# A gated linear attention and a bilinear feed-forward on one core: zero matmuls at the start, half products at the head of two chunks, and a query load behind a gate

## The chip, the cores and the metric

The kernel runs on one core of a Trainium2 chip. The metric is the device time of one launch in microseconds. The kernel of before has a median of 196.31 us over three runs (195.17, 196.31 and 201.79).

The engines are named as the profile names them: PE is TensorE (matmuls) and PEld its weight loads, DVE is VectorE, ACT is ScalarE, POOL is GpSimd, SP is SyncE. POOL, SP and ACT also issue DMA transfers. Each engine runs its own queue of instructions in order and waits at an instruction until what that needs is there.

## The reference

Two stages follow each other. The first is a recurrence over 768 steps for each of 4 batch rows and 8 heads, with a state of 48 x 48:

```python
for t in range(S):
    state = alpha[:, :, t, :, None] * state + np.einsum('bhd,bhe->bhde', k[:, :, t], v[:, :, t])
    y[:, :, t] = np.einsum('bhd,bhde->bhe', q[:, :, t], state)
```

The second takes the 3072 tokens of 384 features and computes `((x @ w_a) * (x @ w_b)) @ w_out`, with an inner width of 1536.

## The kernel before

**Chunks.** The recurrence is cut along time. A chunk is 256 steps of two batch rows: chunk c covers the steps of c // 2 and the batch rows c % 2 * 2 and the next one, so there are six chunks, 0 to 5. Inside a chunk the two batch rows are u = 0 and u = 1, and steps are held in even and odd pairs on 128 partitions.

**Stages of a chunk.** The gates' logarithms (`ln`, L411) are summed over time on TensorE with a triangular matrix: chunk 0 with `B` (L453), chunk 1 with `A2` (L503), the later ones with `AQ` (L498), which takes the sums in three bf16 parts; the parts come from `lx` (L424, L427) and the subtractions `R 0` and `R 1` (L488) on VectorE. ScalarE turns the sums into the decays beta and 1/beta (`E`, L532). `lv` (L517) and `mk`, `mq` (L543) multiply keys and queries by them. The result is turned so that the features lie on partitions: on TensorE for the first chunks (`C`, `Ce`), by a DMA transpose that SP issues for the later ones (`T`, L595, into the tile kqT). Then come the states (`K`, `KA`, L618; `k`, L650 to L654), the scores (`D`, L665) with their masks (`Mc` copies on ScalarE, L674, and `Mm` masks in place on VectorE, L678), and the outputs (`SB`, `SA`, `Y`). For chunks 2 to 5 the output leaves PSUM into ys (`X`, L755 or L757) and is turned by a DMA transpose into xT (`XT`, L762), one for each u.

**Feed-forward.** For a chunk's 512 tokens there are 12 slices f of the inner width. `a f` and `b f` (L777) are three matmuls each into one PSUM bank, `as f` (L783) copies the first out on ScalarE, `pr f` (L791) multiplies both on VectorE. Their second argument says which tokens: `*` both batch rows (512 columns), `0` or `1` one of them (256 columns, which read only that u of xT). The last argument of `a` and `b` is the PSUM bank. `o m h` (L799) are the output matmuls of 128 tokens in two halves of the inner width, `ot` copies them out, `st` stores them.

**Order.** No scheduler runs. The string PROGRAM is a hand written list of such operations, each with its chunk ahead of the colon; the kernel issues them in that order, each to its engine, so that the string fixes the order on every queue. In it the feed-forward of one chunk is interleaved with the attention stages of the next one or two. An instruction that writes a PSUM bank waits until the bank's last reader is done. The copies of `as` rotate through three buffers. All eight banks are addressed by number.

**Loads.** GpSimd issues most loads (`ld ... P`, L404) and the weights (`W`, L384; `Wo`, L387) in the order of the string, with its own small multiplications `lv ... P` between them. SP issues the first loads, the transposes, the stores, and small transfers of decays (`dr`, `dl`, L549, L554).

The operations `fill n i` (n matmuls of 128 x 128 by 512 zero columns into bank i, L437), `c1` (memsets of the zero tile wz and of og, L328 to L331), and `gatet u` (a GpSimd copy of one element of kqT of row u, L851) already exist in the table of operations. Before, `fill` is used twice, with five matmuls behind chunk 0's second sums and with one later, and `gatet` is not used.

Of the kernel before, what the change touches and what calls it, by code (L numbers as in the profile page):

```python
# [14 lines left out]


PROGRAM = """
0: c1a; cz 0 q V; cz 0 b P; cs 0 m P; ci; cz 1 q V; cz 0 v V; ld a 0b Y; ln 0b; cs 0 0 P; cm 0; cu; cu2 P; B 0b 3; Bs 0b; c1; cs 1 m P; ld v 0 P; ld a 1 P
0: cz 1 b P; ld a 0a Y; ln 0a; B 0a 1; Bs 0a; E 0a b; fill 5 2; cus; ld q 0a Y; mq 0a V; E 0b i; ld q 0b Y; ld k 0a Y; ld k 0b Y; mk 0b V; E 0b b; mq 0b V
0: C 0 1 5; E 0a i; mk 0a V; Ce 0 1 V; C 0 0 3; Ce 0 0 V; dk 0 6; fill 1 1; v 0 S; de 0; K 0 0 7; k 0 0 V; ln 1; cs 1 0 P; ld q 1 P; ld k 1 P; W b 0 256  # L20
0: cm 1; ld v 1 P; c2 P; c3 P; D 0 1 5; M 0 1; D 0 0 0; SB 0 6; B 1a 4; Bs 1a; Mc 0 0; Mm 0 0 V; B 1b 5; Bs 1b; E 1a i; E 1a b; mq 1a V; mk 1a V; K 0 1 4; E 1b i
# [117 lines left out]
1: o 0 1 -; ot 0 V; a 1 1 6; a 10 1 1; as 1 1; as 10 1  # L139
3: E 0 b; E 0 i  # L140
1: b 4 1 2; pr 4 1; b 8 1 5; b 1 1 1; a 8 1 6; b 10 1 0; pr 1 1; o 3 0 2; pr 10 1; as 8 1; pr 8 1; o 3 1 -; ot 3 S; st 3 Y
2: a 4 * 7; as 4 *
3: E 1 b
2: a 5 * 6; b 4 * 3
3: E 1 i
1: st 0 Y
3: dr; ld k * P; lv 0 k P; lv 1 k P
4: lx V; R 0
3: mk 0 V; mq 0 V; T 0
4: ld q * Y  # L150
2: a 1 * 2; b 5 * 0; as 5 *; pr 5 *
4: ra 1
2: b 7 * 4; b 10 * 1; pr 4 *; a 10 * 6; as 10 *; pr 10 *
3: mk 1 V
2: a 7 * 0; b 1 * 5; a 0 * 6; b 0 * 7; as 1 *; as 7 *; pr 1 *; pr 7 *; as 0 *; a 3 * 0; b 9 * 1; pr 0 *
3: mq 1 V; ld v * P
5: ld a * P
2: as 3 *; b 3 * 2; a 9 * 6
4: ra 0
2: pr 3 *; as 9 *; pr 9 *; a 2 * 5  # L160
4: lv 0 q P
2: as 2 *; b 2 * 7; pr 2 *
3: KA * 06; D 0 0 4; M 0 0; dl; k * 0 V; k * 1 V
# [21 lines left out]
2: o 2 0 1; o 2 1 -; o 3 0 6; o 1 0 0; o 3 1 -; o 1 1 -  # L185
4: dr
1: st 1 Y
3: a 11 * 5
2: ot 2 V; ot 3 V
4: mq 0 V; mk 0 V  # L190
5: lx V
3: a 9 * 3; a 0 * 2; a 8 * 6; b 11 * 7; as 9 *; as 11 *; as 0 *; pr 11 *; b 9 * 2; b 0 * 1; pr 9 *
5: lv 0 k V
3: as 8 *
2: ot 1 S
3: b 8 * 3; a 5 * 4; as 5 *; a 6 * 6; a 4 * 7; pr 0 *; pr 8 *
5: R 0
4: mq 1 V
3: b 5 * 3; a 1 * 1; pr 5 *; as 4 *; b 6 * 7; as 6 *; pr 6 *
4: ld v * P; K * 0 2; T 0; D 0 1 5  # L200
3: as 1 *
4: D 0 0 3; Mc 0 0; dl; k * 0 V
# [9 lines left out]
4: SB 0 3; SB 1 5; D 1 1 0; Mc 1 1  # L212
3: b 3 * 7; pr 3 *; b 10 * 2
4: D 1 0 0; Mc 1 0; Mm 1 1 V
5: ld q * P; lv 1 q P
3: pr 10 *
4: SA 1; SA 0; Y 0; X 0 S; XT 0
# [738 lines left out]
```

## Time and profile before

| | |
|---|---|
| median of three runs | 196.31 us |
| the profiled execution, its own time | 196.55 us |
| its span | 194.8 us, so 1.75 us lie around it |
| PE busy | 183.4 us, 94% |
| DVE busy | 137.2 us, 70% |
| ACT busy | 103.0 us, 53% |
| POOL busy | 55.8 us, 29% |
| DMA | 30.96 MB, 159 GB/s on average |
| granted TensorE clock | 1.0 |

A row of the timeline gives start, duration, engine, line, operation, what it writes and reads, and in brackets how long the engine had been idle ahead of it and what ended that. A row of the chain that ended last gives start, duration and what held the end at that time. Busy time of PE is modelled, since matmuls are pipelined: the pace is better taken from the start of one group to the start of the next.

### The profile page before, as it was taken

How to read it: one execution, taken by the hardware profiler on the slowest of the kernel's cores; microseconds unless marked ns; L12 is line 12 of the kernel's file. 1: busy time of each engine (PE TensorE's matmuls, PEld its weight loads, DVE VectorE, ACT ScalarE, POOL GpSimd, SP SyncE). 2: the span in 40 equal slices, each digit the busy share in tenths (PEclk: the TensorE clock that was granted, in tenths of full speed). 3: DMA queues.
4: the chain of work that ended last, by engine and by line, in shares of the span. 5: the costliest groups of instructions: out<-in, count | busy, mean ns of one | idle time of the engine just before them, and what ended most of it. 6: DMA issues, size and time to landing. Idle time of an engine off the chain costs nothing.

```text
span 194.8 us, 5851 instructions
## 1 busy us (share of the span) xinstructions
PE 183.4 (94%) x2498; PEld 111.5 (57%) x2498; DVE 137.2 (70%) x230; ACT 103.0 (53%) x189; POOL 55.8 (29%) x75
## 2 busy tenths in 40 slices
PE   1998899899999999999998989999999999999993
PEld 1577675566687877644555534555544556544463
DVE  3588966999899796779979379786755871147520
ACT  4465766686765668555566035766245712154401
POOL 8999734860640424400512400040000000000000
PEclk9999999999999999999999999999999999999999
DMA  5999999999999997999996996566388005013013
GB/s 127 263 214 188 237 231 257 245 247 258 255 228 232 189 252 142 127 267 226 131 237 131 131 277 150 111 51 78 82 156 183 3 3 112 9 43 121 2 40 122
DMA packets 57882, 30.96 MB, mean 159 GB/s; under 512 B 47824, under 2 KB 54880, under 8 KB 57856
## 3 DMA queue, kind: packets, MB, share of 16 engines
q0 software_dynamic: 19680, 18.09, 49.0%
q1 hardware_dynamic: 38032, 12.41, 31.5%
q8 instruction: 19, 0.31, 0.6%
q10 hardware_dynamic: 144, 0.10, 0.2%
q14 instruction: 7, 0.06, 0.1%
HBM read 25.98 MB, written 4.74 MB: 158 GB/s over the span
## 4 chain that ended last, share of the span: by engine, by line
PE 75%; DMA 10%; POOL 8%; issue 2%; DVE 2%; ACT 2%; POOLq 0%; ACTq 0%; DVEq 0%
PE psum L777 43%; PE psum L799 20%; DMA wb_t<-in_moe_w_b_dram 7%; DMA xT<-ys 3%; PE psum L665 3%; PE psum L715 2%; PE psum L618 2%; DVE prod L791 1%; POOL a_t L404 1%; PE psum L498 1%; PE psum L689 1%; PE psum L694 1%; POOL wa_t L384 1%; PE psum L810 1%; POOL v_t L404 1%
## 5 line engine op out<-in xcount | busy, mean ns | idle before, releaser
L777 PE MATMUL psum<-xT,wb_t 128*128 128x512 bf16 (+1 forms) x270 | 57.1, 337 | 0.8 <-DVE prod L791 0.3
L777 PE MATMUL psum<-xT,wa_t 128*128 128x512 bf16 (+1 forms) x270 | 56.1, 337 | 0.7 <-DMA xT<-ys 0.7
L799 PE MATMUL psum<-wo_t,prod 128*128 128x384 bf16 x276 | 48.5, 326 | 0.7 <-issue 0.7
L777 PEld LDWEIGHTS <-wb_t 128*128 128x128 bf16 x270 | 25.6, 98 | 21.6 <-issue 1.1
L777 PEld LDWEIGHTS <-wa_t 128*128 128x128 bf16 x270 | 25.4, 98 | 20.5 <-issue 1.2
L799 PEld LDWEIGHTS <-prod 128*128 128x128 bf16 x276 | 26.2, 98 | 17.6 <-issue 0.7
L517 POOL TENSOR_TENSOR q_t<-q_t,ra 128x384 f32<-128x384 f32 x8 | 9.1, 1135 | 46.8 <-ACT ra L510 32.0
L674 ACT ACTIVATE m<-psum 128x1024 bf16<-128x1024 f32 x16 | 16.2, 1022 | 6.3 <-PE psum L665 6.3
L816 DVE COPY ot<-psum 128x384 f32<-128x384 f32 (+1 forms) x13 | 6.9, 538 | 16.5 <-PE psum L799 14.1
L814 ACT ACTIVATE ot<-psum 128x384 f32<-128x384 f32 (+1 forms) x12 | 5.7, 477 | 12.9 <-PE psum L799 11.9
L678 DVE TENSOR_TENSOR m<-m,mask 128x1024 bf16<-128x1024 bf16 x16 | 11.6, 732 | 0.4 <-ACT m L674 0.4
L543 DVE TENSOR_TENSOR QKp<-k_t,invb 128x768 bf16<-128x768 f32 x10 | 11.1, 1114 | 0.2
L411 ACT ACTIVATE la<-a_t 128x1536 f32<-128x1536 f32 (+2 forms) x9 | 9.5, 1057 | 3.2 <-DMA a_t<-in_alpha_dram 3.1
L670 DVE TENSOR_TENSOR m<-psum,mask 128x1024 bf16<-128x1024 f32 x8 | 9.7, 1218 | 1.6 <-PE psum L665 1.5
L543 DVE TENSOR_TENSOR QKp<-q_t,beta 128x768 bf16<-128x768 f32 x10 | 9.3, 946 | 0.0
L517 POOL TENSOR_TENSOR k_t<-k_t,a_t 128x384 f32<-128x384 f32 x5 | 4.9, 992 | 14.8 <-DMA k_t<-in_k_dram 14.8
L404 POOL DMA_DIRECT2D a_t<-in_alpha_dram x7 | 7.4, 1059 | 5.5 <-DVE prod L791 2.9
L665 PE MATMUL psum<-kqT 64*64 64x128 bf16 x384 | 8.6, 218 | 0.5 <-DVE prod L791 0.2
L453 PE MATMUL psum<-la,ut 128*128 128x192 f32 x16 | 4.7, 448 | 4.2 <-ACT la L411 4.2
L404 POOL DMA_DIRECT2D v_t<-in_v_dram x8 | 8.5, 1066 | 0.1
L665 PEld LDWEIGHTS <-kqT 64*64 64x64 bf16 x384 | 6.4, 107 | 2.9 <-issue 2.5
L755 ACT ACTIVATE ys<-psum 128x768 bf16<-128x768 f32 x7 | 5.6, 809 | 4.3 <-PE psum L694 2.3
(271 smaller groups left out, 274.6 us busy)
## 6 DMA issues: line engine op xcount, KB each, us to landing
out_dram<-ot SPq DMA_DIRECT2D x23, 192.0 KB, 2.6
a_t<-in_alpha_dram POOLq DMA_DIRECT2D x4, 768.0 KB, 11.4
k_t<-in_k_dram POOLq DMA_DIRECT2D x4, 768.0 KB, 8.2
q_t<-in_q_dram POOLq DMA_DIRECT2D x3, 768.0 KB, 10.3
v_t<-in_v_dram POOLq DMA_DIRECT2D x4, 384.0 KB, 6.2
a_t<-in_alpha_dram POOLq DMA_DIRECT2D x3, 384.0 KB, 5.6
q_t<-in_q_dram POOLq DMA_DIRECT2D x3, 384.0 KB, 14.1
k_t<-in_k_dram POOLq DMA_DIRECT2D x3, 384.0 KB, 14.0
```

Of the source, the lines that this page charges most:

```text
L404: eng.dma_start(out=t[:, us, hs].rearrange("p b h r d -> p (b h) (r d)"), in_=src[ch.b0 + us.start:ch.b0 + us.stop, hs, ch.s * 2 * C:(ch.s ...
L411: nc.scalar.activation(out=ch.la[:, us, hs].rearrange("p b h r d -> p (b h r d)"), in_=ch.a[:, us, hs].rearrange("p b h r d -> p (b h r d) ...
L517: eng.tensor_mul(x, x, by)
L543: eng.tensor_mul(QKp[ch.c % 2][:, u, j, :, hs, :D], src[:, u, hs].rearrange("p h r d -> p r h d"), f)
L665: nc.tensor.matmul(s2[g * HC:(g + 1) * HC, r, p, rk, :], lhsT=ch.kqT[u][rs, 1, rk, 2 * h + p, g * HC:(g + 1) * HC], rhs=queriesT(ch, u, 2 ...
L670: nc.vector.tensor_mul(m.rearrange("p r a k s -> p (r a) (k s)"), ch.s2[u, h].rearrange("p r a k s -> p (r a) (k s)"), maskn(4))
L674: nc.scalar.activation(out=m.rearrange("p r a k s -> p (r a) (k s)"), in_=ch.s2[u, h].rearrange("p r a k s -> p (r a) (k s)"), func=AF.Copy)
L678: eng.tensor_mul(x, x, maskn(4))
L777: nc.tensor.matmul(p, lhsT=(wa_t, wb_t)[w][:, kk, f * 128:(f + 1) * 128], rhs=ch.xT[:, us.start // 2:us.stop // 2, kk].rearrange("p u g s ...
L799: nc.tensor.matmul(op, lhsT=ch.prod[:, f, at:at + C], rhs=wo_t[:, f, :], start=(f == 0), stop=(f == NFF - 1))
L814: nc.scalar.activation(out=o_, in_=i_, func=AF.Copy)
L816: eng.tensor_copy(o_, i_)
```

## The change

Three edits, all of them in the string.

1. `c1` moves from behind chunk 0's first sums to the second place of the string, and `fill 7 2` follows it: seven zero matmuls into bank 2 ahead of anything else on TensorE.
2. At the head of chunk 2's feed-forward the products of f = 4, 5 and 1 are made for u = 0 and u = 1 apart, and at the head of chunk 3's those of f = 11, 9 and 0. The bank numbers around them change, and some operations on VectorE change places: `R 0` of chunk 4 goes behind `mq 1` of chunk 3, `lx` of chunk 5 goes behind the first three half products of chunk 3.
3. `gatet 1` of chunk 4 is put on GpSimd's queue ahead of `ld q` of chunk 5.

```diff
-0: c1a; cz 0 q V; cz 0 b P; ... Bs 0b; c1; cs 1 m P; ld v 0 P; ld a 1 P
+0: c1a; c1; fill 7 2; cz 0 q V; cz 0 b P; ... Bs 0b; cs 1 m P; ld v 0 P; ld a 1 P
...
-2: a 4 * 7; as 4 *
+2: a 4 0 7; as 4 0; b 4 0 3
 3: E 1 b
-2: a 5 * 6; b 4 * 3
+2: a 5 0 6; as 5 0; b 5 0 0
 3: E 1 i
 1: st 0 Y
 3: dr; ld k * P; lv 0 k P; lv 1 k P
-4: lx V; R 0
+4: lx V
+2: pr 4 0
 3: mk 0 V; mq 0 V; T 0
 4: ld q * Y
-2: a 1 * 2; b 5 * 0; as 5 *; pr 5 *
+2: a 1 0 5; as 1 0; b 1 0 1; a 4 1 2; b 4 1 3; a 5 1 7; a 1 1 4; pr 5 0; as 4 1; pr 1 0; b 5 1 6; b 1 1 5
 4: ra 1
-2: b 7 * 4; b 10 * 1; pr 4 *; a 10 * 6; as 10 *; pr 10 *
+2: a 10 * 2; as 5 1; b 10 * 1; pr 4 1; pr 5 1; a 7 * 7; as 1 1; as 10 *; pr 1 1; pr 10 *; b 7 * 0; as 7 *
 3: mk 1 V
-2: a 7 * 0; b 1 * 5; a 0 * 6; b 0 * 7; as 1 *; as 7 *; pr 1 *; pr 7 *; as 0 *; a 3 * 0; b 9 * 1; pr 0 *
+2: a 0 * 6; pr 7 *; b 0 * 4; as 0 *; a 3 * 3; b 9 * 5; pr 0 *
 3: mq 1 V; ld v * P
+4: R 0
...
-3: a 11 * 5
+3: a 11 0 5; as 11 0
 2: ot 2 V; ot 3 V
 4: mq 0 V; mk 0 V
+3: b 11 0 7; a 9 0 3; as 9 0; b 9 0 2; a 0 0 4; as 0 0; b 0 0 1; pr 11 0; pr 9 0; pr 0 0
 5: lx V
-3: a 9 * 3; a 0 * 2; a 8 * 6; b 11 * 7; as 9 *; as 11 *; as 0 *; pr 11 *; b 9 * 2; b 0 * 1; pr 9 *
+3: a 11 1 6; as 11 1; b 11 1 7; a 9 1 5; as 9 1; b 9 1 2; a 0 1 3; as 0 1; b 0 1 4; pr 11 1; pr 9 1; pr 0 1
 5: lv 0 k V
-3: as 8 *
+3: a 8 * 6; as 8 *; b 8 * 1; a 5 * 2; as 5 *; a 6 * 3; a 4 * 5; pr 8 *
 2: ot 1 S
-3: b 8 * 3; a 5 * 4; as 5 *; a 6 * 6; a 4 * 7; pr 0 *; pr 8 *
 5: R 0
 4: mq 1 V
-3: b 5 * 3; a 1 * 1; pr 5 *; ...
+3: b 5 * 4; a 1 * 1; pr 5 *; ...
...
 4: D 1 0 0; Mc 1 0; Mm 1 1 V
+4: gatet 1
 5: ld q * P; lv 1 q P
```

More of the change, by code (lines that the diff above doesn't have):

```diff
@@ L17 @@
 PROGRAM = """
-0: c1a; cz 0 q V; cz 0 b P; cs 0 m P; ci; cz 1 q V; cz 0 v V; ld a 0b Y; ln 0b; cs 0 0 P; cm 0; cu; cu2 P; B 0b 3; Bs 0b; c1; cs 1 m P; ld v 0 P; ld a 1 P
+0: c1a; c1; fill 7 2; cz 0 q V; cz 0 b P; cs 0 m P; ci; cz 1 q V; cz 0 v V; ld a 0b Y; ln 0b; cs 0 0 P; cm 0; cu; cu2 P; B 0b 3; Bs 0b; cs 1 m P; ld v 0 P; ld a 1 P
 0: cz 1 b P; ld a 0a Y; ln 0a; B 0a 1; Bs 0a; E 0a b; fill 5 2; cus; ld q 0a Y; mq 0a V; E 0b i; ld q 0b Y; ld k 0a Y; ld k 0b Y; mk 0b V; E 0b b; mq 0b V
@@ L147 @@
 3: dr; ld k * P; lv 0 k P; lv 1 k P
-4: lx V; R 0
+4: lx V
+2: pr 4 0
 3: mk 0 V; mq 0 V; T 0
 4: ld q * Y
-2: a 1 * 2; b 5 * 0; as 5 *; pr 5 *
+2: a 1 0 5; as 1 0; b 1 0 1; a 4 1 2; b 4 1 3; a 5 1 7; a 1 1 4; pr 5 0; as 4 1; pr 1 0; b 5 1 6; b 1 1 5
 4: ra 1
-2: b 7 * 4; b 10 * 1; pr 4 *; a 10 * 6; as 10 *; pr 10 *
+2: a 10 * 2; as 5 1; b 10 * 1; pr 4 1; pr 5 1; a 7 * 7; as 1 1; as 10 *; pr 1 1; pr 10 *; b 7 * 0; as 7 *
 3: mk 1 V
-2: a 7 * 0; b 1 * 5; a 0 * 6; b 0 * 7; as 1 *; as 7 *; pr 1 *; pr 7 *; as 0 *; a 3 * 0; b 9 * 1; pr 0 *
+2: a 0 * 6; pr 7 *; b 0 * 4; as 0 *; a 3 * 3; b 9 * 5; pr 0 *
 3: mq 1 V; ld v * P
+4: R 0
 5: ld a * P
-2: as 3 *; b 3 * 2; a 9 * 6
+2: as 3 *; b 3 * 2; a 9 * 0
 4: ra 0
-2: pr 3 *; as 9 *; pr 9 *; a 2 * 5
+2: pr 3 *; as 9 *; pr 9 *; a 2 * 1
 4: lv 0 q P
@@ L187 @@
 1: st 1 Y
-3: a 11 * 5
+3: a 11 0 5; as 11 0
 2: ot 2 V; ot 3 V
 4: mq 0 V; mk 0 V
+3: b 11 0 7; a 9 0 3; as 9 0; b 9 0 2; a 0 0 4; as 0 0; b 0 0 1; pr 11 0; pr 9 0; pr 0 0
 5: lx V
-3: a 9 * 3; a 0 * 2; a 8 * 6; b 11 * 7; as 9 *; as 11 *; as 0 *; pr 11 *; b 9 * 2; b 0 * 1; pr 9 *
+3: a 11 1 6; as 11 1; b 11 1 7; a 9 1 5; as 9 1; b 9 1 2; a 0 1 3; as 0 1; b 0 1 4; pr 11 1; pr 9 1; pr 0 1
 5: lv 0 k V
-3: as 8 *
+3: a 8 * 6; as 8 *; b 8 * 1; a 5 * 2; as 5 *; a 6 * 3; a 4 * 5; pr 8 *
 2: ot 1 S
-3: b 8 * 3; a 5 * 4; as 5 *; a 6 * 6; a 4 * 7; pr 0 *; pr 8 *
 5: R 0
 4: mq 1 V
-3: b 5 * 3; a 1 * 1; pr 5 *; as 4 *; b 6 * 7; as 6 *; pr 6 *
+3: b 5 * 4; a 1 * 1; pr 5 *; as 4 *; b 6 * 7; as 6 *; pr 6 *
 4: ld v * P; K * 0 2; T 0; D 0 1 5
```

## The prediction

> **What bounds the kernel now.** I read the page's engine shares and clock row first, then the chain of work that ended last in order of time, then the timeline around the three places that are edited, and last the DMA view for the loads that move.
>
> ```profile
> PEclk9999999999999999999999999999999999999999
> PE 75%; DMA 10%; POOL 8%; issue 2%; DVE 2%; ACT 2%; POOLq 0%; ACTq 0%; DVEq 0%
> ```
>
> TensorE carries three quarters of the chain, and the granted clock is full in every slice. The chain in order of time shows where TensorE itself is made to wait:
>
> ```profile
> 17.14 13.55 DMA wb_t<-in_moe_w_b_dram
> 30.69 0.05 issue
> 30.74 1.47 PE psum L777 x6
> ...
> 62.45 5.28 PE psum L777 x48
> ...
> 81.90 11.65 PE psum L777 x54
> ...
> 106.61 6.22 DMA xT<-ys
> 112.83 0.14 issue
> 112.96 9.22 PE psum L777 x42
> ...
> 129.46 0.92 ACT m L674
> 130.38 0.04 issue
> 130.43 0.40 PE psum L665 x14
> ```
>
> Columns are start, duration, what. Up to 30.69 us the chain is loads: the third piece of wb_t, issued at 17.14, sets it. From there on it is matmuls, dense but for a few holes. Two of the holes lie where the change works: the wait for chunk 3's second turned row (to 112.83), and a stretch at 126 to 130.4 where VectorE and ScalarE hold TensorE up. The two L777 rows give the pace: 5.28/48 = 110 ns for a matmul of 256 columns (chunk 1's half products) and 11.65/54 = 216 ns for one of 512.
>
> **Zero matmuls ahead of the first sums.** The memsets of wz and og go to the head of VectorE's queue, and seven 512-column matmuls to the head of TensorE's. The rows of before:
>
> ```profile
> 4.19 2.90 PE L453 MATMUL psum<-la,ut 128*128 128x192 f32 x8 [4.19 <-ACT la L411]
> 6.88 2.15 PE L437 MATMUL psum<-wz 128*128 128x512 bf16 x5
> ```
> ```profile
> 33.87 0.56 DVE L517 TENSOR_TENSOR k_t<-k_t,a_t 128x384 f32<-128x384 f32 x1 [0.85 <-DMA k_t<-in_k_dram]
> ```
>
> TensorE idles until 4.19, and its first matmuls go at half pace although the granted clock reads full: five zero matmuls in 2.15 us are 430 ns each, twice the 216 above, and the first eight sums take 2.90 us. Seven at 430 ns are 3.0 us of the 4.19 idle ones, so they end about when the sums may begin; ahead by a memset, at worst 0.3 us late. If they bring the full pace forward the first sums, and what follows, come half of 2.90, some 1.4 us, sooner (an estimate). I price it at nothing either way. The cover is the 13.55 us row: TensorE still meets wb_t at 30.69, and behind it VectorE meets chunk 1's keys at 33.87, both of them loads that GpSimd issues and that this edit does not touch. The bounds are 0.3 us lost and 1.4 us gained, the latter only if loads do not hold the stage.
>
> [...]
>
> **Row by row products, chunk 2.** Products 4, 5 and 1 of both kinds become halves: six groups of three 512-column matmuls turn into twelve groups of three 256-column ones. Per group split: 6 x 110 - 3 x 216 = +12 ns, so six cost 0.07 us of TensorE. Three evictions on ScalarE and three products on VectorE become six each:
>
> ```profile
> 80.40 0.43 DVE L791 TENSOR_TENSOR prod<-as__1745,psum 128x256 bf16<-128x256 bf16 x1
> ...
> 116.47 0.73 DVE L791 TENSOR_TENSOR prod<-as__2307,psum 128x512 bf16<-128x512 bf16 x1 [1.23 <-PE psum L777]
> ```
>
> That is 2 x 0.43 - 0.73 = 0.13 us on VectorE for each split, some 0.4 in all; ScalarE, with fewer instructions in this stage, pays about the same. It lies beside 11.65 us of dense matmuls. There is no wait of TensorE in front of chunk 2's first product for the split to remove (the dense row starts straight behind the output matmuls), and the row taken first, row 0, is the one whose turn is issued last. Walking the new bank numbers with these durations I find each bank read out before it is written again, the tightest at the scores of chunk 3, whose banks VectorE has free some 0.5 us ahead. R 0 of chunk 4 (one VectorE subtraction) moves behind chunk 3's queries; its reader, chunk 4's quad sums, comes behind all of chunk 2's products. Price 0.07 us; if the cover went, 0.4 us.
>
> **Row by row products, chunk 3.** Here row 0 is turned first.
>
> ```profile
> 103.44 1.99 SPq L762 DMA_TRANSPOSE xT<-ys  x1
> ```
> ```profile
> 112.96 2.75 PE L777 MATMUL psum<-xT,wa_t 128*128 128x512 bf16 x12 [0.68 <-DMA xT<-ys]
> ...
> 128.82 1.50 PE L777 MATMUL psum<-xT,wb_t 128*128 128x512 bf16 x6 [0.33 <-DVE prod L791]
> ...
> 135.38 4.06 PE L799 MATMUL psum<-wo_t,prod 128*128 128x384 bf16 x24
> 139.28 0.81 PE L777 MATMUL psum<-xT,wa_t 128*128 128x512 bf16 x3
> ```
>
> Row 0 is turned from 103.44, row 1 lands at 112.83. The first product reads both and idles 0.68 us; a half product of row 0 does not. TensorE then has six groups (6 x 3 x 110 = 2.0 us) before it needs row 1, which covers it. **Gain 0.68, cost 0.07.** VectorE gains too: it idled 1.23 us until 116.47 because the first second factor came after four first ones; now halves are multiplied at once, its three extra halves (0.4 us) fit into that idle time, and chunk 4's last queries end some 0.8 us sooner. So VectorE keeps step with the earlier TensorE, and I carry the 0.61 through to 126 us.
>
> **Chunk 5's queries behind chunk 4's turned keys.** GpSimd gets a tiny copy that reads chunk 4's second turned tile, and behind it on its queue wait the query load, lv 1 q and the value load of chunk 5, nothing else. Who waits for those: VectorE's lv 0 q and, behind it in order, product 7; later the queries' multiply and the state sums of chunk 5.
>
> ```profile
> 126.05 2.09 DVE L678 TENSOR_TENSOR m<-m,mask 128x1024 bf16<-128x1024 bf16 x2
> ```
> ```profile
> L678 DVE TENSOR_TENSOR m<-m,mask x16: 671/681/1497, 14.0 to 156.6; 128x1024 bf16<-128x1024 bf16 x16
> ```
> ```profile
> 126.16 1.42 POOL L517 TENSOR_TENSOR q_t<-q_t,ra 128x384 f32<-128x384 f32 x1 [16.96 <-ACT ra L510]
> ```
> ```profile
> 121.22 1.94 SPq L595 DMA_TRANSPOSE kqT<-QKp  x1
> 132.64 3.61 SPq L762 DMA_TRANSPOSE xT<-ys  x2
> ```
> ```profile
> kqT<-QKp SPq DMA_TRANSPOSE x2, 4.4
> ```
> ```profile
> q_t<-in_q_dram POOLq DMA_DIRECT2D x1, 768.0 KB, 7.7
> ```
> ```profile
> DMA to landing us min/median/max: 4.3/9.0/15.8
> ```
> ```profile
> 133.42 0.55 DVE L517 TENSOR_TENSOR q_t<-q_t,ra 128x384 f32<-128x384 f32 x1
> 135.65 0.73 DVE L791 TENSOR_TENSOR prod<-as__2470,psum 128x512 bf16<-128x512 bf16 x1 [1.68 <-PE psum L777]
> ```
>
> In times of before: the turn issued at 121.22 lands 4.4 later, at 125.6, and the gate opens; the same load took 7.7 us from issue (the median of query loads is 9.0, the least 4.3, the most 15.8), so the queries land at 133.3. VectorE comes to lv 0 q at 133.42. Product 7 waits for TensorE until 135.65, so lv 0 q may start as late as 135.1: 1.8 us of slack, and no cost.
>
> What it moves is lv 1 q. In before it starts on GpSimd at 126.16, 0.1 us behind two masks on VectorE: the longer took 1497 ns where the median is 681, 0.8 us lost, and product 2 behind them is what TensorE waits for at 128.82 (0.33) and through ScalarE at 130.43. That second wait: six matmuls from 128.82 at 216 ns end at 130.12, the scores start at 130.43, 0.31. With lv 1 q gone to about 133.5 both waits, 0.64 in sum, should go. What is late next is a mask or R 1 near 131 to 134, where its last reader has about 1 us to spare. **Gain between 0 and 0.64; I take 0.5**, as the masks are named by the chain.
>
> [...]
>
> **Sum.** 0.68 - 0.07 - 0.07 + 0.5 = 1.04 us. The profiled execution took 196.55 us, a span of 194.8 and 1.75 around it; the median of the runs is 196.31, 0.24 below it, and its lowest 195.17. 196.55 - 1.04 = 195.5, rounded.
>
> **The rivals.** [...] *The gated load comes late*, the slower side: the point is 135.1 - 125.6 = 9.5 us from issue to landing. Beyond it each microsecond delays lv 0 q, product 7 and TensorE's 24 output matmuls at 135.38, whose eighth (135.38 + 7 x 0.169 = 136.6) reads product 7 (ready 136.4): no slack, one for one. At the median 9.0 nothing happens; at the longest, 15.8, it costs 6.3: 201.8; halfway (12.7) 3.2: 198.7. Against: the queues are quiet then, for it: the median lies only 0.5 below the point. *The value load hits the turns of chunk 4*: behind lv 1 q it is issued at about 134.5, while row 1 is turned from about 135.0. In chunk 3 such a turn beside a value load took 6.22 (106.61 to 112.83) and here it would land at 141.2, 1.9 after 139.28 where TensorE wants it: 197.4. Against: a load's data move some time after its issue, and the turn may be through. *The head pays after all*: the 1.4 us pass 30.7: 194.1. Against: the two loads.
>
> **How the numbers follow.** Forecast 0.42 (own range 194.8 to 196.0), the block moves 0.15, the value load 0.15, the late load 0.17 (0.12 of it beyond +2%, 200.2), the head 0.07, and 0.04 for a gain that no row shows. The range, 193.9 to 198.4, takes in all but most of the late load and the last. Two per cent, 3.9 us, is about what a measurement of this kernel can tell from no change; TensorE's holes after 30.7 us come to less, so faster by over 2% gets 0.04, slower 0.12, within 0.84.
>
> **What would show it.** Right: no wait for xT ahead of chunk 3's first product and VectorE's 1.23 us of idle before its first product there gone; zero matmuls at 1 to 4 us, wb_t still ending at about 30.7; lv 1 q of chunk 5 after 130 us, all masks near 0.68 us at 126, and no wait at the scores of 130.4. Wrong: VectorE waiting for q_t ahead of lv 0 q, TensorE idle behind 135 or ahead of chunk 4's first product, or a first stage that ends before 30 us.

## The result and the profile after

| | before | after |
|---|---|---|
| median on the same chip | 199.05 us, four runs | 198.57 us, four runs (197.22 to 199.54) |
| ratio, after to before | | 1.0135, 95% interval [1.0095, 1.0176] |
| profiled execution, own time and span | 196.55 and 194.8 us | 199.4 and 197.6 us |

Two of the four runs of before (201.79 and 202.78 us) belong to a slower kind of execution that any of these kernels falls into now and then; the ratios leave such runs out, and that is why 1.0135 can stand beside these two medians. The change makes the kernel 1.0 to 1.8% **slower**, some 2.6 us. Two of its own four runs, 199.4 and 199.54 us, have a mean granted clock of 0.991; the two at 1.0 took 197.22 and 197.74, against 195.17 and 196.31 of before. The forecast of 195.5 us was wrong, and so was its range, by 0.17 us at its upper end.

The changed kernel's lines lie three higher, L780 for L777 and so on. Its engine shares and clock row, from the page:

```profile
PE 185.8 (94%) x2541; PEld 115.1 (58%) x2541; DVE 137.6 (70%) x236; ACT 104.4 (53%) x195; POOL 55.6 (28%) x76
PEclk9999999999999999999999999999889999999999
```

PE has the same share as before, and two slices of the 40, from 138 to 148 us, are below full clock. Before had none. The chain that ended last, in order of time, shows how the gain was made and then lost:

```profile
81.22 11.70 PE psum L780 x72
...
112.47 9.11 PE psum L780 x60
...
129.29 0.35 PE psum L668 x16
...
133.83 6.54 DMA xT<-ys
...
140.41 12.87 PE psum L780 x51
```

Against the chain of before: chunk 2's first product 81.90 to 81.22; chunk 3's 112.96 to 112.47, with no wait for xT; the scores of chunk 4 130.43 to 129.29, with neither VectorE nor ScalarE ahead of them. So 1.14 us had been gained by 129.29, against 1.04 forecast. Then come chunk 4's first products, in the chain of before and in that of after the last row above:

```profile
139.44 11.01 PE psum L777 x51
```

They start 0.97 us later than before, at 140.41, and take 12.87 us instead of 11.01.

The timeline of the changed kernel, one engine after the other, shows what came between (start, duration, engine, line, operation, in brackets the idle time ahead and what ended it):

```profile
124.93 0.18 POOL L854 CAST go<-kqT 1x1 f32<-1x1 bf16 x1 [17.25 <-DMA kqT<-QKp]
125.27 1.16 POOL L407 DMA_DIRECT2D q_t<-in_q_dram  x1 [0.16 <-issue]
131.77 1.39 POOL L520 TENSOR_TENSOR q_t<-q_t,ra 128x384 f32<-128x384 f32 x1 [5.33 <-DMA q_t<-in_q_dram]
133.10 1.19 POOL L407 DMA_DIRECT2D v_t<-in_v_dram  x1
```
```profile
131.44 4.03 SPq L765 DMA_TRANSPOSE xT<-ys  x2
```
```profile
134.17 4.06 PE L802 MATMUL psum<-wo_t,prod 128*128 128x384 bf16 x24
140.41 0.82 PE L780 MATMUL psum<-xT,wa_t 128*128 128x512 bf16 x3 [2.17 <-DMA xT<-ys]
```

The gated queries come in good time: issued at 125.27, there at 131.77, 6.5 us later. Behind them lv 1 q ends and the value load is issued at 133.10, 0.73 us ahead of the second of chunk 4's two turns; by the chain that turn takes 6.54 us, from 133.83. TensorE finishes the output matmuls and then stands for 2.17 us.

Windows of 1 us over the same place (busy time of each engine, then the granted clock, the DMA share and GB/s):

```profile
139.00:140.00 1.00, 0.00 (x0) 0.00 (x0) 1.00 (x3) 0.00 (x0) 0.00 (x0) 1.00 1.42 255
140.00:141.00 1.00, 0.59 (x3) 0.31 (x4) 0.82 (x1) 0.00 (x0) 0.00 (x0) 1.00 0.04 14
141.00:142.00 1.00, 1.00 (x5) 0.35 (x3) 0.00 (x0) 0.60 (x1) 0.00 (x0) 0.67 0.80 159
142.00:143.00 1.00, 1.00 (x4) 0.37 (x3) 0.00 (x0) 0.00 (x0) 0.00 (x0) 0.50 1.17 216
```

The DMA share is 1.42 in the window before the turn lands at 140.4 and 0.04 in the one behind. The value load's packets move from 135.0 to 139.7, the turn's from 136.2 to 139.0: both were in flight together. Behind the idle stretch the granted clock is 0.50 from 141.34 to 144.75, and a window holds four matmuls (six in i1 below, at full clock). The 51 matmuls take 12.87 us instead of 11.01, 1.86 more. The ledger closes: 0.97 later and 1.86 longer are 2.83, and the spans differ by 2.8.

### The profile page after: what moved, and what is told of

It is laid out like the page before. It is cut to its first block, busy times and chain, and to the rows that moved or that the text cites. A ratio compares the mean times of both kernels' runs of the same rounds, so it can differ in the third digit from the quotient of the medians.

```text
span 197.6 us, 5968 instructions
## 1 busy us (share of the span) xinstructions
PE 185.8 (94%) x2541; PEld 115.1 (58%) x2541; DVE 137.6 (70%) x236; ACT 104.4 (53%) x195; POOL 55.6 (28%) x76
## 4 chain that ended last, share of the span: by engine, by line
PE 81%; DMA 8%; POOL 6%; issue 2%; DVE 1%; ACT 0%; POOLq 0%; ACTq 0%; DVEq 0%
PE psum L780 47%; PE psum L802 21%; DMA wb_t<-in_moe_w_b_dram 5%; DMA xT<-ys 3%; PE psum L668 3%; PE psum L718 2%; PE psum L621 2%; PE psum L692 2%; PE psum L697 1%; PE psum L813 1%; PE psum L501 1%; POOL v_t L407 1%; POOL a_t L407 1%; PE psum L587 1%; POOL wa_t L387 1%
## 5 line engine op out<-in xcount | busy, mean ns | idle before, releaser
L780 PE MATMUL psum<-xT,wb_t 128*128 128x256 bf16 (+1 forms) x288 | 59.8, 330 | 1.2 <-DMA wb_t<-in_moe_w_b_dram 1.2
L780 PE MATMUL psum<-xT,wa_t 128*128 128x256 bf16 (+1 forms) x288 | 58.5, 329 | 2.3 <-DMA xT<-ys 2.2
L780 PEld LDWEIGHTS <-wa_t 128*128 128x128 bf16 x288 | 27.5, 99 | 21.4 <-DMA xT<-ys 2.6
L780 PEld LDWEIGHTS <-wb_t 128*128 128x128 bf16 x288 | 27.4, 98 | 20.4 <-DMA wb_t<-in_moe_w_b_dram 1.4
L681 DVE TENSOR_TENSOR m<-m,mask 128x1024 bf16<-128x1024 bf16 x16 | 10.8, 683 | 0.3 <-ACT m L677 0.2
L407 POOL DMA_DIRECT2D k_t<-in_k_dram x7 | 7.4, 1061 | 0.0
```

The lines of the kernel that those rows point to most:

```text
L407: eng.dma_start(out=t[:, us, hs].rearrange("p b h r d -> p (b h) (r d)"), in_=src[ch.b0 + us.start:ch.b0 + us.stop, hs, ch.s * 2 * C:(ch.s ...
L681: eng.tensor_mul(x, x, maskn(4))
L780: nc.tensor.matmul(p, lhsT=(wa_t, wb_t)[w][:, kk, f * 128:(f + 1) * 128], rhs=ch.xT[:, us.start // 2:us.stop // 2, kk].rearrange("p u g s ...
```

## The experiments

Runs whose names begin with the same letter (`e` to `i`) shared a chip and its runs of before. Ratios are to before on the same chip; medians count every run. Where an edit is made to the second version below, with both gates, that is said.

**Which load collides: gates taken away and added.** Four kernels.

```diff
e1_no_gate: the change without
-4: gatet 1
e2_gate_only: the kernel before, and only
+4: gatet 1
e4_v_late: the change, and ahead of chunk 5's values a copy of one element of chunk 4's turned row 1
+4: gate xT 1
 5: ld v * P; K * 0 5
e5_fill_wait: the change, and ten zero matmuls
-4: a 7 * 0; ...
+4: fill 10 0; a 7 * 0; ...
```

> The changed kernel without the gate; its queries are loaded as before, the values behind lv 1 q as before. Theory (the gate pushes the value load into the turn of chunk 4's row 1): the wait of 2.2 us ahead of chunk 4's first product and the half clock behind it both go; what the other edits brought by 128 us (some 0.5 us) stays, the masks at 126 are blocked again: span 193.9 to 194.9, time 195.7 to 196.7, ratio to before 0.995 to 1.0. Rival (the half products or the zero matmuls cost the time, by the clock or the banks): half clock or a wait of about 2 us stays, time 198 to 199.5.

> The kernel of before with the gate alone. Theory: masks at 126 unblocked (0.5 us gained), then row 1 of chunk 4 lands some 6.5 us after its issue in place of 2.8, TensorE waits about 2 us, and if that idle stretch trips the clock another 1.8 us: time 197.8 without and 199.7 with the half clock. Rival (the other edits cost it): no wait, 195.5 to 196.5.

> The changed kernel with chunk 5's value load behind a second gate, which reads chunk 4's turned row 1, so that no load runs beside that turn; the query gate stays. Theory: row 1 lands about 2.8 us after issue, no wait, no half clock, and the 1.2 us that the change had gained by 133 us stay: span 193.4 to 193.9, time 195.2 to 195.7. Rival (the gated query load or lv 1 q is what delays chunk 4): the wait stays, 197.5 to 199.5.

> The changed kernel with ten zero matmuls (2.2 us) put where TensorE waits for chunk 4's turned row 1. Theory: the wait is still there in length (the row lands at 140.4), but TensorE is busy in it and the clock does not halve: every run at a granted clock of 1.0, span 195.4 to 196.0, time 197.2 to 197.8. Rival (the half clock comes from how hard TensorE has worked before, not from the idle stretch): clock below 1 as often as in the changed kernel, up to 199.5.

Medians of four runs each: e1 200.46 us (197.7 to 203.71), e2 196.05 (195.34 to 198.71), e4 195.19 (194.88 to 197.08), e5 198.49 (197.96 to 199.56). No ratios were formed here. The runs at a mean granted clock of 0.998 or more compare like with like: before 195.46 and 196.22, e1 197.7 and 198.62, e2 195.34 to 196.32, e4 all four, e5 197.96 to 199.0.

**e4** answers the question. POOL's timeline and the chain:

```profile
131.52 1.44 POOL L521 TENSOR_TENSOR q_t<-q_t,ra 128x384 f32<-128x384 f32 x1 [5.29 <-DMA q_t<-in_q_dram]
136.81 0.78 POOL L851 CAST go<-xT 1x1 f32<-1x1 bf16 x1 [3.85 <-DMA xT<-ys]
137.54 1.20 POOL L408 DMA_DIRECT2D v_t<-in_v_dram  x1
```
```profile
134.14 3.90 PE psum L803 x24
138.04 11.01 PE psum L781 x51
```

With the value load held until the turn has landed, the turn is there at 136.81, the first product follows the output matmuls without a hole, and its 51 matmuls take 11.01 us. Everything else is as in the change. Against the 198.57 of the change, on another chip, some 3 us come back.

**e2** missed: I expected the wait there too. Its two turns are issued as early as in the change, but the values later:

```profile
131.24 3.65 SPq L763 DMA_TRANSPOSE xT<-ys  x2
```
```profile
135.37 1.19 POOL L405 DMA_DIRECT2D v_t<-in_v_dram  x1
```

The second turn goes out at 133.66 (133.83 in the change), and the load comes 1.71 us behind it instead of 0.73 ahead of it; the turn takes 2.8 us and no wait appears. So the gate alone does not bring the collision about; what differs here is the order of these two issues. The load is late because the gate opens at 126.46 instead of 124.93, although the turn of chunk 4's keys that it reads is issued as early (120.41 against 120.60). Counted by its semaphore in the traces, that turn takes 5.7 to 6.0 us in before, e2, f2, f3 and h3 and 4.2 to 4.8 in all the others. In the five slow cases a 16 KB packet of the DMA queue that the page calls `instruction` starts while the turn ends, at 124.1 to 125.2. In the others it starts within 0.6 us of the turn's issue. No run tested whether the packet is what holds the turn up.

**e1** did not answer its question, since its profiled execution collided elsewhere: the ungated query load, issued at 107.41, met chunk 3's second turn, issued at 107.72. The chain:

```profile
107.72 12.69 DMA xT<-ys
```

That execution took 203.71 us, the longest of the four, so 12.69 us is an instance of what loads can do to a turn, and no price. But its runs at full clock, 197.7 and 198.62 us, are no faster than the change: taking the gate away alone does not give the time back, and where these two lose it no trace shows.

**e5** was meant to take the half clock away and leave the wait. The collision is there again: the load is issued at 134.28, 0.25 us ahead of the turn, and the turn lands at 140.47 by its semaphore, 5.9 us after its issue. TensorE was done with the output matmuls at 139.72 and would have waited 0.8 us; the zeros (2.16 us on the chain) cover that and cost some 1.4 more. With a wait of 0.8 us in place of 2.17 the run does not test the half clock. Inconclusive.

**The parts of the change, one at a time,** each taken out of the version with both gates (e4):

```diff
f1_no_head:      c1 back behind Bs 0b, no fill 7 2
f2_no_rows3:     the head of chunk 3 as before
f3_no_rows2:     the head of chunk 2, and R 0 of chunk 4, as before
f4_no_query_gate: no gatet 1
```

> The kernel with both gates, with its head as before (memsets of wz and og behind chunk 0's first sums, no zero matmuls ahead). Theory (the head pays about 0.6 us, as the chain reached chunk 1's state sums at 37.6 in place of 38.3 us): span 194.0 to 194.2, time 0.6 above the kernel with both gates (195.2), so 195.7 to 196.0. Rival (the prediction's: loads hold the first 34 us, so the head is worth nothing): 195.0 to 195.4.

> The kernel with both gates, chunk 3's first products whole again. Theory: the wait for the second turned row comes back (0.5 to 0.7 us) and VectorE starts its products later: span 194.0 to 194.8, time 195.8 to 196.6. Rival (with the query load gone from beside it, row 1 lands early enough for whole products): 195.0 to 195.3.

> The kernel with both gates, chunk 2's first products whole again and R 0 at its old place. Theory (halves there only cost 12 ns a group): span 193.3 to 193.4, time 195.0 to 195.3. Rival (they free VectorE in a stage that it nearly fills): 195.6 or more.

> The kernel with the value gate but without the query gate: chunk 5's queries go out beside the turn of chunk 3's row 1 and the turns of chunk 4's keys. Theory (a load's 4224-byte packets hold up a turn's 256-byte ones): row 1 of chunk 3 lands more than 6 us after its issue, in some executions 12 or more; where it is more than 8 TensorE waits up to 6 us ahead of the products of row 1 and the clock halves after that wait: 195.5 to 196 where it is short, 200 to 204 where it is long. Rival (the query gate only moved lv 1 q off the masks): 195.5 to 196 in every execution.

| | median of ten, all counted | ratio to before |
|---|---|---|
| f1 | 195.92 us | 1.0003 [0.9958, 1.0048] |
| f2 | 196.36 us | 1.0024 [0.9964, 1.0084] |
| f3 | 197.13 us | 1.0055 [1.0011, 1.0098] |
| f4 | 196.94 us | 1.0054 [1.0021, 1.0088] |

f1, PE's timeline at the start, and the same stretch of the change:

```profile
4.18 2.90 PE L457 MATMUL psum<-la,ut 128*128 128x192 f32 x8 [4.18 <-ACT la L415]
6.87 2.34 PE L441 MATMUL psum<-wz 128*128 128x512 bf16 x5
```
```profile
1.20 3.17 PE L440 MATMUL psum<-wz 128*128 128x512 bf16 x7 [1.20 <-DVE og L332]
4.18 1.84 PE L456 MATMUL psum<-la,ut 128*128 128x192 f32 x8
5.86 1.24 PE L440 MATMUL psum<-wz 128*128 128x512 bf16 x5
```

The head does bring the full pace forward, 1.84 us for the eight sums instead of 2.90. But f1 without it reaches chunk 1's state sums at 37.65, the change with it at 37.60. The 1 us is lost in the stage that waits for loads. f4 has the long masks again:

```profile
125.19 2.09 DVE L681 TENSOR_TENSOR m<-m,mask 128x1024 bf16<-128x1024 bf16 x2
```

and reaches chunk 4's first product at 138.59 against 138.04 with the gate: 0.55 us for the query gate. f2's chain begins chunk 3's products without a wait for xT:

```profile
112.52 9.06 PE psum L781 x42
```

That is 0.25 us later than e4's 112.27, and a hole at 104.6 that is longer by 0.38 (1.46 us against 1.08) would make up more than that. In f2 whole products find the turned row there: it lands at 110.34 by its semaphore, with chunk 4's value load issued behind the turn (109.22 against 107.59). That does not make the half products idle where the load goes first. In the change it is issued at 106.50, ahead of the turn at 107.53, and the turn takes 6.41 us and lands at 113.95, 1.5 us after the first product; in e4 it lands at 113.80. There the products of row 0 cover the wait, with the queries gated too. f3's loss is not that of the half products alone, since in its profile the late value load ran into chunk 5's key turns:

```profile
144.06 5.45 DMA kqT<-QKp
```

**The change and the second gate again, and a turn put late without any load.**

```diff
g4_change_again: the change
g3_v_late_again: e4
g1_late_turn: e4, and chunk 2's store of row 1 nine times over ahead of the turn
-4: Y 1; X 1 S; XT 1
-2: st 1 Y
+4: Y 1; X 1 S
+2: st 1 Y; ... (nine)
+4: XT 1
g2_late_turn_filled: g1, and fill 13 0 ahead of chunk 4's first product
```

> The kernel with both gates, with nine issues of one output store (the same rows, written again) on SP ahead of chunk 4's second turn, so that this turn goes out about 4 us later and TensorE must wait 2 to 3.5 us ahead of chunk 4's first product, with no load in play. Theory (an idle stretch of this length is what halves the clock): a granted clock near 0.5 for some 3 us right behind the wait in the profile or in most runs (mean clock 0.98 to 0.992), time 195.2 + wait + 1.8, so 199 to 200.5 with it and 197.5 to 198.7 without. Rival (the clock fell in the changed kernel for another reason, the load's traffic or the work before): 197.5 to 198.7 at a clock of 1.0 in every run.

> The same, with 13 zero matmuls (2.8 us) on TensorE in that wait. Theory: no idle stretch, the clock stays at 1.0 in every run, 197.8 to 198.8, below the kernel without them by up to 1.8 where that one's clock fell. Rival: the clock falls as often as without them.

> The kernel with both gates once more, beside the change and before on one chip. Theory: 195.0 to 195.8, 2 us or more below the change. Rival (the first four executions were a lucky draw and the values, loaded later, meet the turns of chunk 5's keys): 196.5 to 197.5.

> The change once more on that chip. Theory (the value load and the turn of chunk 4's row 1 start within about 2 us of each other, and a few tenths decide which is first): some executions at 195.2 to 195.8 without the wait, the others at 197.2 to 199.6. Rival (the collision is certain): none under 197.

g3 195.47 us, ratio 0.999 [0.9957, 1.0024]; g4 198.51 us, 1.0128 [1.008, 1.0175]. The second gate is worth the 3 us on another chip too. g4's chain has the collision again,

```profile
134.68 6.30 DMA xT<-ys
...
141.03 9.02 PE psum L780 x41
```

with a wait of 1.94 us, but 9.02/41 = 220 ns is full pace: no half clock behind it. So the wait belongs to the change, the half clock only to some executions.

g1 (212.9 us) and g2 (212.25 us) overshot. Stores of the same rows went one after the other, 1.86 us each, and the idle stretch became 15.74 us, 10.9 with zeros. They show only that the granted clock fell to 0.50 in idle stretches of these two lengths. Windows of g1, whose TensorE stands from 139.2 to 155.0:

```profile
142.00:144.00 2.00, 0.00 (x0) 0.00 (x0) 0.00 (x0) 0.00 (x0) 0.00 (x0) 0.98 0.27 98
144.00:146.00 2.00, 0.00 (x0) 0.00 (x0) 0.00 (x0) 0.00 (x0) 0.00 (x0) 0.50 0.27 98
...
158.00:160.00 2.00, 2.00 (x6) 0.69 (x5) 0.00 (x0) 0.00 (x0) 0.00 (x0) 0.50 0.76 65
160.00:162.00 2.00, 2.00 (x8) 0.82 (x7) 0.00 (x0) 1.19 (x2) 0.00 (x0) 0.76 1.56 151
```

In g1 the clock falls about 5 us after TensorE stopped and comes back about 6 us after it resumed.

**What remained open: the short stretch, the place of the load, the gates alone.**

```diff
h1_turn_two_late: as g1, with two stores; i1_turn_three_late: three; i2_turn_four_late: four
h2_turn_two_late_filled: h1, and fill 11 0 ahead of chunk 4's first product
h3_gates_only: the kernel before, and only
+4: gatet 1
 5: ld q * P; lv 1 q P
+4: gate xT 1
 5: ld v * P; K * 0 5
h4_v_first: the change, with the values ahead of the gate (no second gate)
+5: ld v * P
 4: gatet 1
-5: ld v * P; K * 0 5
+5: K * 0 5
```

> The version with both gates (values too), with the turn of chunk 4's row 1 put behind two stores of row 1 of chunk 2's output instead of ahead of one (the extra store writes the same rows again). A store of the same rows took 1.86 us in the earlier run, so the turn is issued about 3 to 4 us later, and TensorE should idle 2 to 3 us ahead of chunk 4's first product with no load beside the turn. Theory (an idle stretch of about 2 us is enough for the half clock): a granted clock near 0.5 for 3 us behind the stretch, and a time of 195.5 + 2.5 + 1.9 = about 200. Rival (the stretch alone is not enough; the half clock needs something more than 2 us): full clock behind it, time about 198.

> The same, with eleven zero matmuls of 512 columns (2.4 us) on TensorE ahead of chunk 4's first product, so that TensorE is busy while it waits. Theory: no half clock, so about 198, that is 1.9 less than the version without zeros. Rival: the same time as without zeros, 198 for both.

> The kernel before with the two gates alone (queries of chunk 5 behind chunk 4's turned keys, values of chunk 5 behind chunk 4's turned output); no zero matmuls at the start, no half products. Theory (the gates make the difference, and the half products are worth at most 0.5 us): 195.3 to 196.3, and no query load beside chunk 3's turn, so no wait of several us ahead of chunk 3's first product. Rival (half products and zeros are needed too): 197 or more.

> The change with one load moved: chunk 5's values are issued ahead of the gate instead of behind lv 1 q. Theory (the value load's place behind lv 1 q makes the wait at chunk 4): no wait ahead of chunk 4's first product, but the load now runs at about the time of chunk 3's or chunk 4's key turns, and may delay these: 195.5 if not, up to 199 if it sits beside chunk 3's second turn as the query load did. Rival (the wait at chunk 4 does not come from the value load): 2 us of wait there as in the change, 198.5.

> As the run with two stores ahead of the turn of chunk 4's row 1, but with three. With two the turn was issued at 136.13 and TensorE did not wait; each further store of the same rows puts it back by some 1.9 us, so TensorE should idle about 1.9 us ahead of chunk 4's first product. Theory (an idle stretch of 2 us is enough for the half clock): granted clock near 0.5 for some 3 us behind it, 197 + 1.9 + 1.7 = about 200.5. Rival (2 us is too short for that by itself): full clock, about 199.

> The same with four stores: some 3.8 us of idle time. Theory and rival differ in the one before; here both expect the half clock if the limit lies under 3.8 us: 197 + 3.8 + 1.7 = 202.5 with it, 200.8 without it.

| | median | ratio to before |
|---|---|---|
| h1 | 197.04 us | 1.0033 [0.9995, 1.0072] |
| h2 | 198.54 us | 1.0147 [1.0065, 1.0229] |
| h3 | 196.09 us | 0.9979 [0.9943, 1.0014] |
| h4 | 196.79 us | 1.0039 [1.0, 1.0079] |
| i1 | 198.64 us | 1.0112 [0.9999, 1.0225] |
| i2 | 202.69 us | 1.0324 [1.022, 1.0428] |

**h4** fits the theory: the value load only moved ahead of the query load, and the wait at chunk 4 is gone (chain):

```profile
139.57 10.57 PE psum L781 x49
```

So the place of the value load alone makes that wait. By its ratio h4 gives back about 1% of the change's 1.3%; it lies 0.4% above before where g3 lies level with it, and that rest is not explained. **h3**, the two gates and nothing else of the change, measures the same as the whole with both gates (0.9979 against 0.999, intervals that overlap almost wholly). In its chain the queries take 8.08 us behind the gate and end on the critical path:

```profile
126.75 8.08 DMA q_t<-in_q_dram
```

lv 0 q starts at 134.86, 0.2 us short of the 135.1 beyond which the prediction lets the late load cost time. **h1** made no idle time, the turn landed as the output matmuls ended; **h2** therefore paid for its zeros, and neither says anything of the clock. **i1** and **i2** do. i1's chain has the same turn with no load beside it:

```profile
138.47 2.75 DMA xT<-ys
```

2.75 us against the 6.54 of the change. PE's idle time in i1, then in i2, from their timelines, and a window behind each:

```profile
141.27 0.82 PE L782 MATMUL psum<-xT,wa_t 128*128 128x512 bf16 x3 [1.90 <-DMA xT<-ys]
```
```profile
142.00:143.00 1.00, 1.00 (x6) 0.42 (x5) 0.00 (x0) 0.60 (x1) 1.00 (x1) 1.00 0.66 133
```
```profile
143.52 0.82 PE L782 MATMUL psum<-xT,wa_t 128*128 128x512 bf16 x3 [3.31 <-DMA xT<-ys]
```
```profile
145.00:146.00 1.00, 1.00 (x6) 0.49 (x5) 0.00 (x0) 0.03 (x1) 0.41 (x1) 1.00 1.14 214
```

After 1.90 us and after 3.31 us of idleness the clock is full in these executions. The length of the stretch alone does not explain the half clock of the change's profile, where 2.17 us went before it.

In the change the clock falls at 141.34, 3.1 us after TensorE stopped at 138.24 and 0.93 us after it went on; in i2 TensorE stops at 140.21 and the clock reads 1.00 in every window to 152. What set the half clock off is not shown by these traces.

## Why the prediction was wrong

**The step that failed** is the pricing of the query gate at no cost: the sum has no term for the value load that the same gate holds back. I asked who waits for the queries and found 1.8 us of slack; that was right, the queries were early. I named the value load's collision with the turn of chunk 4 as a rival, worked it out, and gave it 0.15 instead of putting it into the sum. Its working came out: a turn at about 6.2 us beside a load (6.54 and 6.30 measured), a landing at 141.2 (140.4 and 141.0), a wait of 1.9 (2.17 and 1.94), a time of 197.4 (medians of 198.57 and 198.51, the least run 197.05). What made me discount it, "a load's data move some time after its issue, and the turn may be through", holds in e2, where the turn is issued first, and not in the change: there the load, issued at 133.10, moves its packets from 135.0 to 139.7, the turn from 136.2 to 139.0. The row that should have decided stood in the prediction: chunk 3's turn beside a value load took 6.22 us, twice the 2.75 of a turn by itself in i1.

That the rival came out so closely is in part luck. Its time of issue, 134.5, rests on a landing of the gating turn 4.4 us after its issue. That figure belongs to chunk 4's other key turn; the one meant took 5.96 us in before, by its semaphore. With 5.96 the load would have been issued at about 136.1, behind the turn at 135.0, as in e2. In the change the gating turn took 4.3 us, for a reason the prediction did not have.

**The half clock was in no term.** It added 1.86 us in the profiled execution. The change's two runs at full clock lie within the range, the two at 0.991 above it; g4's profile had the wait with full clock behind it, and its four runs at full clock go from 197.05 to 198.96. The half clock does not belong to the change alone: of the 82 executions of before beside the experiments, 42 have a mean granted clock of 0.992 or less, and each of these took at least 198.19 us, the others at most 197.2. What sets it off is **not settled by a run**: i1 and i2, at full clock behind 1.90 and 3.31 us of idleness, rule out the length of the idle stretch as the only condition. The clock is low near the start as well: 0.59 from 10 to 15 us in g4 and 0.50 from 12 to 16 us in i1.

**Terms that held.** Head: priced at 0, and f1 shows no loss without it. Chunk 2's halves: priced at -0.07; no loss shows, f3 cannot give the size. Chunk 3's halves: 0.68 less 0.07 priced; the wait did go, and in the change the halves covered it, since row 1 landed 1.5 us after the first product. In f2, where the turn goes ahead of the value load, there is no wait to cover, so the term is no fixed gain. Masks: 0.5 priced, 0.55 by f4, one execution each. Two masks took 1.27 us in the change as forecast, and lv 1 q met lv 0 q instead,

```profile
132.22 1.35 DVE L520 TENSOR_TENSOR q_t<-q_t,ra 128x384 f32<-128x384 f32 x1
```

which is 1.35 us where before it was 0.55; it cost the chain nothing. lv 1 q runs on GpSimd from 131.77 to 133.16 beside it, as it ran from 126.16 beside the mask of 1497 ns before. So VectorE was held up in another place instead, by 0.80 us, to which the prediction gives 0.15 as the block that moves; the 0.5 was gained all the same.

**The gain in the runs.** With both gates the profiled spans are 193.4 and 193.5 us against 194.8, the forecast gain and a little more. The runs do not show it: 0.999 [0.9957, 1.0024] for g3. The sum was made against one execution of before, 196.55 us, while the runs of before that the comparisons use go from 194.77 to 197.2. A gain of 1 us against one execution is within that spread.

**The better version** is e4, which is g3: 3.0 us faster than the change and level with before. No version here is shown to beat before in the comparisons.

## What to carry to other kernels

When an instruction in an in-order queue is made to wait, price each transfer queued behind it at its new time of issue, together with the stage as it will run after the rest of the change, and ask which transpose is in flight then. Here a turn of 2.75 us became one of 5.9 to 6.5 us when the value load was issued within a microsecond ahead of it, and the wait of about 2 us that followed in the change was more than the other edits had gained together. If a late load can wait, gate it on the landing of the turn that it would meet.

## What the runs showed of the hardware that was not expected

**A hole with no cause in the profile.** "issue" at or ahead of the second part of chunk 3's outputs (L718 in the change) is on the chain of most kernels here, whatever was changed around it: 1.39 us in the change at 104.64, 1.08 in e4, 1.46 in f2, 0.65 in h1 and 1.69 in g4, the last being the same kernel as the change. TensorE waits there for nothing that the profile shows. It varies by 1 us between kernels that do the same work around it, as much as the whole forecast gain. In all twenty traces it ends 1.2 to 1.6 us after a 16 KB packet of the `instruction` queue (at 104.65 in the change, 105.41 in g4), while its start moves between 104.0 and 106.6. No run tested whether the two belong together, so the cause stays open.

**A turn's price went by the order of issue.** Over chunk 3's and chunk 4's second turns in all traces, nine that were issued 0.2 to 1.0 us behind a value load took 5.6 to 6.8 us; nine issued 1.5 to 2.2 us behind one took 4.4 to 6.0; four issued at least 0.4 us ahead of it took 2.8 to 4.0. Those with no load near, at chunk 4, took 2.7 to 4.4. The chunk 3 turns of before (0.25 us ahead of the first of two loads, 6.22) and of e1 (12.69) lie outside this count.

**The clock row says nothing of the first microseconds.** At the start of f1 eight sums take 2.90 us and five zero matmuls 2.34 (468 ns each) with the row at 1.0; after seven zeros the same sums take 1.84 and the five zeros 1.24 (248 ns). The prediction read this as half pace at a full clock. The traces have no clock record that early: the first one, of full clock, starts at 8.72 us in before, 9.08 in f1 and 4.81 in the change, and the row counts what has no record as 1.0. At 142 to 144 us the row does read 0.50 at the same pace.
